# First values loaded from the ScalarE queue, the second batch's casts between the output weights, and the first output blocks three at a time

## The chip, the core and the metric

The kernel runs on one core of a Trainium2 chip. The metric is the device time of one execution in microseconds. Five engines run side by side, each through its own instructions in a fixed order: TensorE (PE in the rows; its weight loads are PEld), VectorE (DVE), ScalarE (ACT), GpSimd (POOL) and SyncE (SP). They wait for one another, and for DMA transfers, through semaphores. A transfer is issued by an instruction that stands in the order of the engine that issues it.

## The reference

Attention over 8 batches, 8 heads, 576 positions and 64 values per head: heads 0 to 3 see the last 32 positions, heads 4 to 7 every fourth of the last 128. Then a two-layer network on the 4608 rows of 512.

```python
scores = scale * np.matmul(q, k.transpose(0, 1, 3, 2))
mask_plain = (rel >= 0) & (rel < window)
mask_dil = (rel >= 0) & (rel < window * dilation) & (rel % dilation == 0)
scores = np.where(masks[None, :, :, :], scores, -1000000000.0)
attn = np.exp(scores); attn = attn / (np.sum(attn, axis=-1, keepdims=True) + 1e-09)
out = np.matmul(attn, v)
...
h = x @ w_in
g = h * (1.0 / (1.0 + np.exp(-beta * h)))
return (g @ w_out).astype(np.float32)
```

## The kernel before

The work is written in the order in which each engine gets it; nothing reorders it. A **batch** is brought in by steps that run on DMA. `cast_qk` (issued by GpSimd) reads q or k as float32 and writes a bfloat16 copy to a scratch in memory. `load_dil` and `load_plain` (issued by SyncE) read that copy transposed into `kdT`, `qdT` (heads 4 to 7), `kpT`, `qpT` and `opT` (heads 0 to 3). `load_vd` (2 transfers) and `load_vp` (8 to 10 transfers) bring the values as float32 into `vd_st` and `vp_st`, of which there is one each, and `cast_v` copies them into `vd` and `vp`. `spread_dil`, `spread_k` and `spread_q` copy the transposed q and k into the zero-padded tiles `qzd`, `kz` and `qq`.

The **attention** of a batch is a list of 33 steps, `STEPS`. `S` steps are scores and their exponential (`pt`, ScalarE, line 291), `V` steps are the product with the values and its division (PE line 307, VectorE lines 310 and 314), and `X` steps transpose the result into `xT` (PE line 323, ScalarE lines 329 and 333). The first figure behind the letter is the pair of heads: 2 and 3 are the dilated heads, whose steps come first; 0 and 1 are the plain ones. V00 is the first step that reads `vp`, V20 the first that reads `vd`. For batches 0 and 1 the mask is added on PE as a first matmul; from batch 2 on GpSimd multiplies it in after the exponential (line 293).

The **network** runs over 9 tiles of 512 rows, t = 0 to 8, in slots. `slot_h(t, fb)` is four 512-column matmuls, a tanh on ScalarE (line 351) and a product on VectorE (line 354) that gives `g`. `slot_o(t, tb, part)` is four of the sixteen 512-column matmuls of the output block `tb`; after part 3 ScalarE copies the block to `osb` (line 382) and SyncE stores it two slots later. Tile t = 0 uses batch 0 alone, and after its 16 h slots come its 16 o slots, block by block. The attention of batch t + 1 is laid between the slots of tile t: `FROM[t]` is the first slot behind which steps may stand, and slots weigh 1 (h) or 2 (o), except the last two, which weigh nothing. `extras(b)` hangs the loads and spreads of a batch on steps of the attention of batch b.

Hardware DMA transfers take eight semaphores in turn, and a ninth transfer waits until the first has landed; the transfers that GpSimd issues have eight of their own. Of PSUM's eight banks `psum_at` has five, `psum_h` two and `psum_o` one, and the `osb` pool has two buffers.

The start of the program before is written out by hand:

```python
    cast_v(0, 1, G)
    for n in range(2):
        spread_dil(0, n, nc.vector)
        spread_k(0, n, G)
    cast_v(0, 0, G)
    for g in range(4):
        load_w_in(g)
    for g in range(4):
        load_w_out(g)
```

After it come the steps of batch 0, then `build_beta`, then the casts and loads of batch 1.

## Time and profile before

| | us |
|---|---|
| median of 3 runs | 374.37 (373.09 to 481.56) |
| profiled execution, its own time | 375.59 |
| span of its trace | 373.9 |
| PE busy in the span | 315.0 (84%) |
| VectorE, ScalarE, GpSimd busy | 207.5, 189.7, 129.8 |

The trace is of one execution. Times in it are counted from the start of the span, and some 1.7 us of the execution lie outside the span. PEclk in a table by windows is the clock granted to TensorE as a share of 2.4 GHz: 1.00 is 2.4 GHz and 0.50 is 1.2 GHz. The share of busy time is an average over stages with different limits, so the stages are looked at one by one.

### The profile page before, as it was taken

What the parts mean: (1) busy time and instruction counts of PE and PEld (TensorE: products, weight loads), DVE (VectorE), ACT (ScalarE), POOL (GpSimd) and SP (SyncE); (2) the same over time, 40 slices, a digit from 0 to 9 for tenths busy, and PEclk for the clock granted to TensorE, in tenths of its full rate; (3) what the DMA queues carried; (4) which work ended last, traced back from release to release, by engine and by line L of the source; (5) the groups of instructions that cost most, each with busy time, mean ns of one, the idle gap of its engine ahead of it and who ended that gap; (6) DMA issues with size and microseconds to landing.
All of it is one profiled execution on the core that took longest, in us unless ns stands there. A gap on an engine that the chain in (4) does not pass through costs nothing.

```text
span 373.9 us, 5943 instructions
## 1 busy us (share of the span) xinstructions
PE 315.0 (84%) x2173; PEld 162.2 (43%) x2173; DVE 207.5 (55%) x421; ACT 189.7 (51%) x360; POOL 129.8 (35%) x162
## 2 busy tenths in 40 slices
PE   0267997487469499989999998999899999999995
PEld 0144443253235245545554554555455544444442
DVE  4353650644698827955894698479555634425400
ACT  1164652055446247656665675566566645535511
POOL 8837100210545634465355346424453300000000
PEclk9995899769989879999999999999999999999999
DMA  7948999899989779249927983996100110010022
GB/s 134 222 111 134 199 223 216 197 177 179 218 151 220 148 160 240 66 95 174 251 62 156 169 220 79 176 212 157 38 24 27 34 52 29 28 58 29 28 72 70
DMA packets 91262, 48.93 MB, mean 131 GB/s; under 512 B 74832, under 2 KB 86112, under 8 KB 90720
## 3 DMA queue, kind: packets, MB, share of 16 engines
q1 hardware_dynamic: 86176, 34.91, 41.6%
q0 software_dynamic: 5056, 13.63, 20.5%
q8 instruction: 17, 0.28, 0.3%
q14 instruction: 13, 0.11, 0.1%
HBM read 40.89 MB, written 18.87 MB: 160 GB/s over the span
## 4 chain that ended last, share of the span: by engine, by line
PE 55%; DVE 19%; DMA 11%; SPq 6%; ACT 3%; issue 2%; POOL 1%; DVEq 0%; ACTq 0%; POOLq 0%
PE h_ps L346 24%; PE o_ps L377 23%; DMA qk<-in_q_dram 7%; DVE qq L224 5%; DVE g L354 5%; DVE xs L314 4%; DVE kz L216 3%; SPq L237 2%; DMA w_in_bf<-in_moe_w_in_dram 2%; ACT tnh L351 2%; PE h_ps L377 2%; PE at L323 2%; SPq L203 2%; PE at L307 2%; SPq L192 1%
## 5 line engine op out<-in xcount | busy, mean ns | idle before, releaser
L354 DVE SCALAR_TENSOR_TENSOR g<-tnh,h_ps 128x512 bf16<-128x512 bf16 x134 | 91.3, 684 | 95.4 <-ACT tnh L351 95.3
L377 PE MATMUL o_ps<-w_out_bf,g 128*128 128x512 bf16 x544 | 139.0, 386 | 4.9 <-ACT osb L382 4.9
L346 PE MATMUL h_ps<-xT,w_in_bf 128*128 128x512 bf16 x536 | 137.3, 386 | 6.7 <-DVE g L354 5.7
L351 ACT ACTIVATE tnh<-h_ps,beta_half 128x512 bf16<-128x512 f32 x134 | 92.1, 687 | 64.8 <-PE h_ps L346 62.3
L346 PEld LDWEIGHTS <-w_in_bf 128*128 128x128 bf16 x576 | 54.0, 100 | 61.5 <-issue 12.7
L377 PEld LDWEIGHTS <-g 128*128 128x128 bf16 x576 | 53.5, 99 | 59.5 <-issue 9.4
L291 ACT ACTIVATE pt<-at 128x288 bf16<-128x288 f32 (+1 forms) x112 | 48.7, 443 | 42.6 <-PE at L285 30.1
L293 POOL TENSOR_TENSOR pt<-pt,mask_d 128x288 bf16<-128x288 bf16 x48 | 34.8, 733 | 55.3 <-ACT pt L291 55.3
L314 DVE TENSOR_TENSOR xs<-at,rcp 72x256 bf16<-72x256 f32 (+1 forms) x96 | 44.6, 465 | 13.2 <-PE at L323 8.9
L382 ACT ACTIVATE osb<-o_ps 128x512 f32<-128x512 f32 x34 | 20.3, 597 | 39.1 <-PE o_ps L377 32.5
L293 POOL TENSOR_TENSOR pt<-pt,mask_PP 128x384 bf16<-128x384 bf16 x24 | 24.2, 1008 | 34.1 <-ACT pt L291 34.0
L307 PEld LDWEIGHTS <-pt 128*128 128x128 bf16 x448 | 26.3, 103 | 22.0 <-issue 8.4
L253 POOL CAST vd<-vd_st 128x2048 bf16<-128x2048 f32 x8 | 16.1, 2013 | 44.2 <-DMA vd_st<-in_v_dram 44.2
L323 PE MATMUL at<-ident_b,xs 72*128 72x72 bf16 (+1 forms) x224 | 20.1, 210 | 13.0 <-DVE xs L314 5.5
L307 PE MATMUL at<-vd,pt 128*128 128x65 bf16 x256 | 19.8, 202 | 6.1 <-POOL vd L253 3.6
L285 PEld LDWEIGHTS <-kdT 128*128 128x128 bf16 x128 | 13.2, 106 | 27.1 <-issue 16.5
L323 PEld LDWEIGHTS <-xs 72*128 72x128 bf16 (+1 forms) x224 | 14.1, 103 | 22.5 <-DVE xs L314 12.6
L285 PE MATMUL at<-qzd,kdT 128*128 128x144 bf16 x128 | 19.9, 244 | 4.3 <-DVE qzd L212 4.3
L310 DVE RECIPROCAL rcp<-at 72x4 f32<-72x4 f32 (+1 forms) x96 | 17.0, 178 | 11.3 <-PE at L307 10.4
L329 ACT COPY xT<-at 128x288 bf16<-128x288 bf16 x32 | 12.6, 399 | 17.8 <-PE at L323 17.7
L271 PE MATMUL at<-neg_d,ident_b 128*128 128x288 bf16 x16 | 6.1, 385 | 14.7 <-DVE neg_d L154 14.7
L277 PE MATMUL at<-qq,kz 128*128 128x96 bf16 x192 | 16.7, 212 | 1.2 <-ACT qq L224 1.1
(63 smaller groups left out, 197.6 us busy)
## 6 DMA issues: line engine op xcount, KB each, us to landing
vp_st<-in_v_dram SPq DMA_DIRECT2D x62, 96.0 KB, 4.0
vd_st<-in_v_dram SPq DMA_DIRECT2D x8, 512.0 KB, 5.9
qk<-in_k_dram POOLq DMA_DIRECT2D x6, 576.0 KB, 5.9
qk<-in_q_dram POOLq DMA_DIRECT2D x6, 576.0 KB, 8.9
vd_st<-in_v_dram SPq DMA_DIRECT2D x8, 384.0 KB, 4.7
w_in_bf<-in_moe_w_in_dram POOLq DMA_DIRECT2D x4, 512.0 KB, 8.3
w_out_bf<-in_moe_w_out_dram POOLq DMA_DIRECT2D x4, 512.0 KB, 16.3
out_dram<-osb SPq DMA_DIRECT2D x8, 256.0 KB, 2.7
```

The costliest lines, as they stand in the source:

```text
L224: copy_on(eng)(out=qq[b % 2][rows, :, :, e], in_=raw[b, kind][rows, c0:c0 + 2 * S].rearrange("p (h i u) -> p h i u", h=4, i=NI))
L285: nc.tensor.matmul(sc[:, a, 0:2 * n], lhsT=kd[b][:, rp, h4, hf * (CT - P):hf * (CT - P) + P], rhs=qzd[b % 2][:, :, rp, h4, hf * HT:(hf + 1 ...
L291: nc.scalar.activation(out=w, in_=sc[:, :, 0:2 * n], func=ACT.Exp, scale=SCALE)
L293: nc.gpsimd.tensor_tensor(out=w, in0=w, in1=mask, op=ALU.mult)
L307: nc.tensor.matmul(pv[:, a, h2, :], lhsT=pt[x][:, c:c + P], rhs=rhs, start=True, stop=True)
L314: nc.vector.tensor_tensor(out=xs_t[b, x, jx][:, a0:a0 + m], in0=pv[0:n, :, :, 0:D], in1=rcp[0:n, 0:m].unsqueeze(3).to_broadcast([n, m, 2, ...
L323: nc.tensor.transpose(xp[:, a * n:(a + 1) * n], xs[:, a].rearrange("p h d -> p (h d)"), ident_b[0:n, 0:n])
L346: nc.tensor.matmul(hps, lhsT=w_in_bf[:, kt, fb * P:(fb + 1) * P], rhs=xT[:, kt, t * NTOK:(t + 1) * NTOK], start=(kt == 0), stop=(kt == NKT ...
L351: nc.scalar.activation(out=tnh[:], in_=hps, func=ACT.Tanh, scale=beta_half[:, fb:fb + 1])
L354: nc.vector.scalar_tensor_tensor(out=g[:], in0=tnh[:], scalar=1.0, in1=hps, op0=ALU.add, op1=ALU.mult)
L377: nc.tensor.matmul(ops[:], lhsT=g_t[t, fb][:, tb * P:(tb + 1) * P], rhs=w_out_bf[:, fb, :], start=(fb == 0), stop=(fb == NFB - 1))
L382: nc.scalar.mul(out=osb[:], in_=ops[:], mul=0.5)
```

## The change

The loads of batch 0's values and of `beta` are issued by ScalarE ahead of its first activation. The dilated half of batch 0's values is cast by VectorE. The dilated masks are built before the plain ones, and four memsets of `kz` go from GpSimd to VectorE. Two of the four groups of `w_in` are issued before the cast of `vp`. The values of batch 1 are loaded ahead of its transposes, and its q and k are cast between the second and third group of `w_out`. The first three output blocks of t = 0 run part by part, in the two banks of `psum_h` and the one of `psum_o`. `FROM` goes from 26 to 27 and from 5 to 8, `osb` from two buffers to four, and the rows of `vp` and `vd` from 96 to 66 elements. Batch 2's casts stand behind a one-element GpSimd copy that reads batch 1's `opT`, at V22 instead of V31, and its loads at V23 instead of X31.

```diff
-    FROM = {0: 26, 1: 5}
-    DV = 96
+    FROM = {0: 27, 1: 8}
+    DV = D + 2
...
-    osb_pool = pool("osb", 2)
+    osb_pool = pool("osb", 4)
...
-            nc.gpsimd.memset(kz[i][64:128, :, :, 0], 0.0)
-            nc.gpsimd.memset(kz[i][0:64, :, :, 1], 0.0)
+            nc.vector.memset(kz[i][64:128, :, :, 0], 0.0)
+            nc.vector.memset(kz[i][0:64, :, :, 1], 0.0)
...
-            if t == NTT - 1 and tb % 2:
+            if t == NTT - 1 and tb % 2 or t == 0 and tb < 2:
                 o_t[t, tb] = psum_h.tile([P, HD], FP32, name="h_ps")
...
+            if b == 1:
+                at("V22", wait_raw, 1)
             for kind in "kq":
-                at("S20" if b > 1 else "V31", cast_qk, b + 1, kind)
+                at("S20" if b > 1 else "V22", cast_qk, b + 1, kind)
             for kind in "kq":
-                at("V21" if b > 1 else "X31", load_dil, b + 1, kind)
+                at("V21" if b > 1 else "V23", load_dil, b + 1, kind)
...
+    def wait_raw(b):
+        G.tensor_copy(out=gate_t[0:1, 0:1], in_=raw[b, "o"][0:1, 0:1])
...
+    load_vd(0, A)
+    load_vp(0, A)
+    A.dma_start(out=beta_row[:], in_=moe_beta.rearrange("(f p) -> f p", p=P))
     make_identity(nc, ident_b[:])
+    build_masks_d()
+    build_masks_p()
     zeros()
...
+    cast_v(0, 1, V)
+    for n in range(2):
+        spread_dil(0, n, V)
+        spread_k(0, n, G)
+    finish_masks_p()
     make_identity(nc, ident_f[:])
...
+    for g in range(2):
+        load_w_in(g)
     cast_v(0, 0, G)
-    for g in range(4):
+    for g in range(2, 4):
         load_w_in(g)
...
+    load_vd(1, SQ)
+    load_vp(1, SQ)
+    for g in range(2):
+        load_w_out(g)
+    for h in (4, 0):
+        for kind in "kq":
+            cast_qk(1, kind, h, 4)
+    for g in range(2, 4):
+        load_w_out(g)
...
+        if t == 0:
...
+            left = [(slot_o, 0, tb, part) for part in range(4) for tb in range(3)] + left[12:]
```

The order of ScalarE's instructions at the start of the program shows the first two parts of this. Names in brackets are semaphores that an instruction waits for: DMAHW0 to DMAHW7 are the eight of the hardware queues, DMASW0 to DMASW7 those of GpSimd's transfers. Before:

```order
L109 ACT_TABLE_LOAD
L109 ACTIVATE warm<-warm 128x1 [waits DVE_49]
L291 ACTIVATE pt_115<-at 128x288 [waits PE_49] x4
L291 ACTIVATE pt_116<-at 128x288 [waits PE_49] x3
L224 COPY qq_109<-qpT 64x24x48 [waits DMAHW5_49]
```

ScalarE loaded its table at once and had nothing else ahead of the first exponential. The same engine in the changed program, from the seventh of its thirteen transfers on:

```order
L245 DMA vp_st<-in_v_dram 64x6x64 [waits DMAHW2_49]
L245 DMA vp_st<-in_v_dram 64x6x64 [waits DMAHW4_49]
L245 DMA vp_st<-in_v_dram 64x6x64 [waits DMAHW5_49]
L245 DMA vp_st<-in_v_dram 64x6x64 [waits DMAHW6_49]
L245 DMA vp_st<-in_v_dram 64x6x64 [waits DMAHW7_49]
L245 DMA vp_st<-in_v_dram 64x6x64 [waits DMAHW0_49]
L442 DMA beta_row<-in_moe_beta_dram 16x128 [waits DMAHW1_49]
L112 ACT_TABLE_LOAD
L112 ACTIVATE warm<-warm 128x1 [waits DVE_49]
L295 ACTIVATE pt_115<-at 128x288 [waits PE_49] x4
```

Thirteen transfers, the table load and the warm-up now stand ahead of the first exponential. The semaphores are shared with SyncE's transposes: DMAHW4 was last taken by `qdT`, DMAHW7 by `kpT` and DMAHW1 by `qpT`, so the transfer of `beta` waits until `qpT` has landed.

GpSimd's order, from the cast of `vp` on, before:

```order
L164 DMA w_in_bf<-in_moe_w_in_dram 128x4x512 x4
L169 DMA w_out_bf<-in_moe_w_out_dram 128x4x512 [waits DMASW0_49]
L169 DMA w_out_bf<-in_moe_w_out_dram 128x4x512 [waits DMASW1_49]
L169 DMA w_out_bf<-in_moe_w_out_dram 128x4x512 [waits DMASW2_49]
L169 DMA w_out_bf<-in_moe_w_out_dram 128x4x512 [waits DMASW3_49]
L180 DMA qk_463<-in_k_dram 16x9216 [waits DMASW4_49]
L180 DMA qk_463<-in_q_dram 16x9216 [waits DMASW5_49]
L180 DMA qk_463<-in_k_dram 16x9216 [waits DMASW6_49]
L180 DMA qk_463<-in_q_dram 16x9216 [waits DMASW7_49]
```

And in the changed program, from the third and fourth group of `w_in` on:

```order
L172 DMA w_in_bf<-in_moe_w_in_dram 128x4x512 x2
L177 DMA w_out_bf<-in_moe_w_out_dram 128x4x512 [waits DMASW0_49]
L177 DMA w_out_bf<-in_moe_w_out_dram 128x4x512 [waits DMASW1_49]
L188 DMA qk_226<-in_k_dram 16x9216 [waits DMASW2_49]
L188 DMA qk_226<-in_q_dram 16x9216 [waits DMASW3_49]
L188 DMA qk_226<-in_k_dram 16x9216 [waits DMASW4_49]
L188 DMA qk_226<-in_q_dram 16x9216 [waits DMASW5_49]
L177 DMA w_out_bf<-in_moe_w_out_dram 128x4x512 [waits DMASW6_49]
L177 DMA w_out_bf<-in_moe_w_out_dram 128x4x512 [waits DMASW7_49]
```

The four casts of batch 1 moved ahead of the last two groups of `w_out`, so these two land after them.

## Rows read from the trace of the kernel before

**Rows 1.** Busy time by stage (window, length, then each engine's busy us and instructions).

```profile
core 0: us, PE busy (x) PEld busy (x) DVE busy (x) ACT busy (x) POOL busy (x), PEclk, DMA share, GB/s
0.00:17.08 17.08, 0.40 (x2) 0.21 (x2) 6.70 (x26) 1.49 (x2) 13.99 (x30) 1.00 0.91 173
...
29.05:34.57 5.52, 4.22 (x55) 3.31 (x54) 3.06 (x9) 3.20 (x8) 5.52 (x8) 0.56 0.83 122
34.57:50.84 16.27, 16.26 (x64) 6.80 (x65) 9.54 (x14) 10.07 (x15) 2.50 (x6) 0.83 1.23 201
50.84:62.24 11.40, 10.03 (x47) 4.39 (x45) 2.19 (x5) 2.12 (x4) 0.00 (x0) 1.00 1.10 203
62.24:87.30 25.06, 16.02 (x160) 10.51 (x158) 10.95 (x31) 8.93 (x23) 4.41 (x5) 0.80 0.94 196
...
96.56:133.67 37.11, 25.94 (x197) 13.38 (x197) 28.57 (x48) 15.58 (x33) 21.06 (x23) 0.89 0.87 177
```

**Rows 2.** Waits of PE, 0 to 134 us: us in total, times, longest us.

```profile
PE at L285 <- DVE qzd L212: 4.3, 2, 2.3
...
PE at L307 <- POOL pt L293: 2.5, 2, 2.1
```

**Rows 3.** Timeline of the opening (start, length, engine, line; in brackets the idle time before).

```profile
0.80 1.28 ACT L109 ACT_TABLE_LOAD   x1 [0.80 <-PEq L512]
...
4.73 0.91 DVE L119 MEMSET vd_st<- 32x1024 f32 x1 [0.25 <-issue]
...
14.35 2.46 SPq L203 DMA_TRANSPOSE qpT<-qk  x1
...
17.52 1.85 ACT L291 ACTIVATE pt<-at 128x288 bf16<-128x288 f32 x4 [15.21 <-PE at L285]
...
25.02 0.61 SPq L438 DMA_DIRECT2D beta_row<-in_moe_beta_dram  x1
...
28.95 3.03 POOL L164 DMA_DIRECT2D w_in_bf<-in_moe_w_in_dram  x4
29.05 0.34 PE L307 MATMUL at<-vp,pt 128*128 128x65 bf16 x6 [3.34 <-POOL vp L251]
```

**Rows 4.** DMA issues: the q transpose issued at 14.35 us, the last weight issued by 34.2 us.

```profile
qpT<-qk SPq DMA_TRANSPOSE x1, 4.8
...
w_in_bf<-in_moe_w_in_dram POOLq DMA_DIRECT2D x1, 512.0 KB, 5.6
...
w_out_bf<-in_moe_w_out_dram POOLq DMA_DIRECT2D x1, 512.0 KB, 19.0
```

**Rows 5.** Chain that ended last, in order of time: sixteen 512-column matmuls back to back.

```profile
359.06 3.45 PE h_ps L377 x16
```

**Rows 6.** Timeline of the second batch's attention: the waits and what ends them.

```profile
67.15 0.30 PE L307 MATMUL at<-vd,pt 128*128 128x65 bf16 x4 [3.65 <-POOL vd L253]
...
68.43 1.91 PE L377 MATMUL o_ps<-w_out_bf,g 128*128 128x512 bf16 x4
...
72.07 4.36 SPq L366 DMA_DIRECT2D out_dram<-osb  x5
...
75.03 0.60 ACT L382 ACTIVATE osb<-o_ps 128x512 f32<-128x512 f32 x1 [5.94 <-DMA out_dram<-osb]
...
75.97 0.40 PE L323 MATMUL at<-ident_b,xs 72*128 72x72 bf16 x4 [4.55 <-ACT pt L291]
```

**Rows 7.** Timeline of the third batch's start: slots of t = 1, VectorE copy and GpSimd queue.

```profile
66.29 1.79 DVE L216 COPY kz<-kpT 64x1536 bf16<-64x1536 bf16 x2 [3.86 <-DMA kpT<-qk]
...
89.83 1.89 PE L346 MATMUL h_ps<-xT,w_in_bf 128*128 128x512 bf16 x8 [0.64 <-DVE g L354]
...
92.34 1.89 PE L346 MATMUL h_ps<-xT,w_in_bf 128*128 128x512 bf16 x8 [0.63 <-DVE g L354]
...
97.38 1.89 POOL L253 CAST vd<-vd_st 128x2048 bf16<-128x2048 f32 x1 [20.96 <-DMA vd_st<-in_v_dram]
...
100.19 5.68 DVE L216 COPY kz<-kpT 64x1536 bf16<-64x1536 bf16 x2
```

More of the change, by code (lines that the diff above doesn't have):

```diff
@@ L108, in zeros @@
         nc.vector.memset(warm[:], 0.0)
+        nc.vector.memset(vd_st[96:128, 0], 0.0)
+        for e in range(2):
+            nc.vector.memset(vp_st[64 * e:64 * e + WIN // 2, 0, 0], 0.0)
         nc.scalar.activation(out=warm[:], in_=warm[:], func=ACT.Exp)
@@ L114, in zeros, with negate, build_masks_d, build_masks_p @@
             nc.vector.memset(qzd[i][0:64, 1], 0.0)
-            nc.gpsimd.memset(kz[i][64:128, :, :, 0], 0.0)
-            nc.gpsimd.memset(kz[i][0:64, :, :, 1], 0.0)
+            nc.vector.memset(kz[i][64:128, :, :, 0], 0.0)
+            nc.vector.memset(kz[i][0:64, :, :, 1], 0.0)
             nc.vector.memset(vp[i][:, :, :, D:D + 1], 1.0)
             nc.vector.memset(vd[i][:, :, :, :, D:D + 1], 1.0)
-        nc.vector.memset(vd_st[96:128, 0], 0.0)
-        for e in range(2):
-            nc.vector.memset(vp_st[64 * e:64 * e + WIN // 2, 0, 0], 0.0)
-    def build_masks():
-        pp = mask_p["PP"]
+    def negate(n, m):
+        nc.vector.tensor_scalar(
+            out=neg[n][:], in0=m, scalar1=-1.0, scalar2=NEG, op0=ALU.add, op1=ALU.mult)
+    def build_masks_d():
+        for hf, lo in ((0, 0), (1, HT - 16)):
+            flat = mask_d[hf][:].rearrange("p a b n -> p (a b) n")
+            nc.gpsimd.memset(flat, 1.0)
+            nc.gpsimd.affine_select(
+                out=flat, in_=flat, pattern=[[0, 4], [1, HT]], base=lo,
+                channel_multiplier=-1, compare_op=ALU.is_ge, fill=0.0)
+            nc.gpsimd.affine_select(
+                out=flat, in_=flat, pattern=[[0, 4], [-1, HT]], base=WIN - 1 - lo,
+                channel_multiplier=1, compare_op=ALU.is_ge, fill=0.0)
+            negate(f"d{hf}", mask_d[hf][:].rearrange("p a b n -> p a (b n)"))
+    def build_masks_p():
+        pp, fp = mask_p["PP"], mask_p["FP"]
         for e in range(2):
@@ L236, in load_vp, with load_vd @@
                 if b or h4:
[L237 removed]
+                    eng.dma_start(out=dst, in_=src(0, 0))
                 else:
[L239 to L242 removed]
+                    eng.dma_start(out=dst[:, 1:NI], in_=src(1, 0))
+                    eng.dma_start(out=dst[WIN // 2:64, 0:1], in_=src(0, WIN // 2))
+    def load_vd(b, eng):
         rows = v[b, 4:8].rearrange("h (t T) d -> t h (T d)", T=C)
         st = vd_st[:].rearrange("p f h T d -> p f h (T d)")
[L245 to L246 removed]
+        eng.dma_start(out=st[0:96, 0], in_=rows[0:96])
+        eng.dma_start(out=st[:, 1], in_=rows[16:CT])
     def cast_v(b, h, eng):
@@ L452 @@
             for n in range(4):
-                spread_q(0, n, nc.vector if n % 2 else nc.scalar)
+                spread_q(0, n, V if n % 2 else A)
         attention_step(0, name)
     build_beta()
-    for h in (4, 0):
-        for kind in "kq":
-            cast_qk(1, kind, h, 4)
     for kind in "kq":
         load_dil(1, kind)
-    load_vd(1)
     for kind in "kqo":
         load_plain(1, kind)
-    load_vp(1)
     at_once = [4, 2] + [1] * (NTT - 3) + [4]
```

63 lines of the change are left out of this document (18 added, 45 removed).

## The prediction, made before the changed kernel ran

> **What bounds the kernel now.** I read the table by stages first, since 84% busy on PE hides where it is idle. From 134 us on PE is near its bound and the change touches little there; what can be won lies before. The table [rows 1] shows four places. Batch 0's attention ends with 5.52 us at a PEclk of 0.56. The h slots of t = 0 take 16.27 us at 0.83, so part of them runs at 1.2 GHz. The stretch from 62.24 to 87.30, batch 1's attention, holds only 16.02 us of PE work in 25.06. The attention of batch 2 takes 37.11 us with PE at 25.94 and VectorE at 28.57.
>
> The timelines then say what ends each wait. In batch 0, V00 starts 3.34 us late because `vp` is cast late [rows 3]; its loads stand last on SyncE's queue, and `beta`, behind them, is issued at 25.02. In batch 1 PE waits 3.65 us for the cast of `vd`, and then 4.55 us in a longer chain [rows 6]: PE waits for an exponential, which stands on ScalarE behind an `osb` copy, which waits 5.94 us for a store of an earlier block, and that store, at 72.07, was queued on SyncE behind the loads of `vp`. In batch 2 PE waits for `qzd` (4.3 us in two waits over this whole stretch, the longest 2.3) and 2.1 us for GpSimd's masking [rows 2], because GpSimd's queue stood still for 20.96 us until `vd_st` had landed at 97.38 [rows 7].
>
> **The change part by part.** I write A to E for five stages in order of time, a minus for time won.
>
> *A, to the first h slot (34.57 before).* Moving the values to ScalarE's queue takes V00's wait away but puts a new one in. ScalarE is an in-order engine: its first exponential now stands behind thirteen transfers, and the last of them, `beta`, waits until `qpT` has landed; then come the table load of 1.28 us and the warm-up. Before, the table was loaded at 0.80 and the first exponential ran at 17.52 [rows 3]. `qpT` was issued at 14.35 and landed 4.8 us later, at 19.15 [rows 3, 4]. Two `vd` issues leave SyncE's queue ahead of it; at the 0.61 us of a like issue [rows 3] that is 1.2 us, so 17.9. Against that the values now share the DMA engines with the casts from the start. At most all 0.77 MB of `vp` get ahead of `qpT`, at the opening's 173 GB/s [rows 1] 4.4 us, so 22.3. I take 18.5, near the lower end, since `vd` had stood ahead of `qpT` before too. With the issue of `beta` (0.61) and the table load (1.28) ScalarE is free at 20.4, 2.9 us later than the old first exponential (2.3 to 6.7). VectorE is not later: its memsets grow by four at 0.9 us each (the nearest row is the 0.91 of `vd_st`, rows 3) and by a cast that takes GpSimd 1.89 [rows 7]; from the masks at an estimated 7 us through 5.1 us of old memsets this ends near 18.5 with the spreads.
>
> V00 could have run at 29.05 less 3.34, at 25.7; 2.9 later is 28.6, 0.4 earlier than now. So of the 3.3 us almost all is given back. The tail from 29.05 to 34.57 is 5.52 us of which PE worked 4.22 at 0.56; GpSimd now issues `w_in` before the cast of `vp`, some 8 us earlier, so nothing waits for weights, and I take 0.9 off. A is -1.3, between -2.3 and +4.
>
> *B, the sixteen h slots.* PE's low clock followed the idle 3.3 us. Without that I expect 2.4 GHz: sixteen matmuls take 3.45 us [rows 5], a slot of four 0.863, sixteen slots 13.8 against 16.27. B is -2.5, between -2.5 and 0.
>
> *C, the output blocks up to the attention of batch 1.* Three blocks in three banks need no wait for an `osb` copy between them. Twelve parts are 12 x 0.863 = 10.4 us, against 11.40 for eleven parts with their gaps. C is -1.0. Its risk is the weights, since the last two groups of `w_out` come after the four casts. Before, the first group landed 5.6 us after its issue at 28.95, and the eighth 19.0 after its issue at 34.2 [rows 3, 4], so seven groups took 18.6 us, 2.66 each. A cast of half the heads is 288 KB beside the 512 of a group, 1.5 us. `w_in` is now issued when GpSimd has copied `kz`, near 20.4 (`kpT` at 17 and about 3 us), so the first group lands at 26.0 and the last at 26.0 + 18.6 + 4 x 1.5 = 50.6. Batch 1's values, 1.66 MB at the weights' rate (1.05 MB of float32 in 2.66 us), add up to 4.2: 54.8. The last round needs it at 33.3 + 13.8 + 9 x 0.863 = 54.9. So it is just in time; each us that the weights are later costs one. C is between -1.0 and +4. The transposes of batch 1 start when its first cast lands (44 with all delays); the first two are in by 44 + 2 x 2.46 + 4.8 = 53.7, before 57.5, where S20 now stands.
>
> *D, the attention of batch 1 with the last o slots (25.06).* Its values are loaded some 25 us ahead, so the 3.65 go. With four `osb` buffers no copy of t = 0 waits for a store, so the 4.55 go. One o slot that cost 1.91 at the low clock [rows 6] is counted in C now. 25.06 less 10.1 leaves 15.0. What comes late next is the chain of the steps itself. Three `osb` copies ahead of the exponentials may cost 0.6 each, and the slots at full clock may win 1 us each: D is -10.1, between -8.3 and -12.
>
> *E, tile t = 1 (87.30 to 133.67, 46.4 us).* `FROM` at 8 puts three more h slots ahead of the attention. Alone, two slots take 2.51 us (89.83 to 92.34, rows 7), so three cost 3.8, less 3 x 0.69 of VectorE time that leaves the crowded part: +1.7. Batch 2's casts wait only for `opT` of batch 1, near 57 to 61, not for the late cast of `vp`, so the 2.3 us for `qzd` go; and with `vd_st` early GpSimd's queue is empty when masking starts, so the 2.1 go. E is -2.7, between +2 and -7. The rest, t from 2 on, stays as it is; narrower `vp` rows are read by the same matmuls, and I put them at nothing.
>
> The sum is -1.3 - 2.5 - 1.0 - 10.1 - 2.7 = -17.6. From the profiled execution's own 375.6 us that gives 358. That execution is 1.2 us above the median of 374.4, a spread I leave in the range.
>
> **Where the skill and the rows meet.** The table copies of `kz` on VectorE took 5.68 us for batch 2 and 1.79 for batch 1 [rows 7], the slow ones while GpSimd masked its backlog. The Trainium skill, page "SBUF — State Buffer", section "Who interferes with whom", says that a VectorE copy in a two-port mode and a GpSimd instruction exclude each other for whole instructions; the trace agrees as far as it goes. By that rule an empty GpSimd queue would also give back the 3.9 us between the two rows, and the sum would be 354.
>
> The first values now come over another engine's queue, and the opening's DMA share is already 0.91 [rows 1]. The Trainium skill, page "DMA: Bandwidth & Descriptors", section "Issuing engines are not separate DMA queues", says that issuing from several engines saves only sequencer time, since all share the same 16 engines. By that rule the move alone gains no bandwidth and could only shift what waits; my A, where 0.4 of 3.3 us is left, is of that kind.
>
> **The rivals.** *Weights late.* If GpSimd's `w_in` issue slips by 3 us or the casts and transposes share worse, PE waits in the third and fourth round of C, 4 us, and after such a wait the clock may fall as it did after 3.34 us: 1.9 instead of 0.86 for some slots. That costs C 5 and D 1 or so: 364. For it speaks that the margin is 0.1 us; against it that the first round of blocks needs only the first group.
>
> *ScalarE held longer.* If `qpT` lands at 22.3, the first exponential runs at 24.2, A is +2.5 and the weights, issued after `kz`, move with it: 362 to 365. For it speaks the shared DMA in the opening; against it that SyncE's own queue got shorter.
>
> *VectorE's copies run free.* `kz` and `qq` of batch 2 at their short times, as the 1.79 of batch 1: E is -6.6, 354. Against it: GpSimd still masks each exponential there.
>
> *Slower.* One mechanism could turn the sign: ScalarE's hold with no bound. Each us that `qpT` lands later delays the first exponential, and with it everything, by one. The gain is used up when `qpT` lands 17.6 us later than I take, at 36; with all 2.6 MB of both batches' values ahead of it at 173 GB/s (15 us) and SyncE's issues stretched with them it would land at 38 to 42, and the time is 378 to 382. Against it: batch 1's values stand behind `opT` on SyncE.
>
> *It doesn't do what it says.* V00's wait may only move from `vp` to ScalarE; I hold this for most of A already. If PE then idles long enough at the start of the attention to lose the clock again, B is 0 as well: 361.
>
> **How the numbers follow.** I give my sum 0.55, weights late 0.14, ScalarE held longer 0.12, copies running free 0.10, the clock lost again 0.05, slower 0.04. The range goes from 351 (free copies and D at its end) to 367 (weights late and ScalarE held together). A measurement of this kernel tells about 2% from no change, 7.5 us: below 366.9 is faster. Only the two middle rivals together, and the slower one, come above: faster 0.87, same 0.09, slower 0.04. I predict 358.
>
> **What would show it.** In the changed profile: the first exponential near 20.4, ending a wait of ScalarE that goes back to `beta` and `qpT`; no wait for `vp` at V00; h slots of t = 0 at 0.863; `o_ps` and `h_ps` blocks without gaps, S20 of batch 1 near 58; no wait for `vd` or a store behind it, t = 1 beginning near 72.5; t = 1 in 44 us. If the first exponential is past 24, or PE waits for `w_out_bf`, or t = 1 takes over 48, the step named there is wrong.

## The result, and the profile after

The changed kernel takes 360.36 us (median of 4 runs, 359.55 to 360.58) against 374.44 us before: a ratio of 0.963 (95% interval 0.960 to 0.966), 14.1 us less. The prediction was 358, in a range of 351 to 367. The profiled run took 360.58 us with a span of 358.9; before it was 375.6 and 373.9.

The table of stages of the changed kernel, cut at the marks that [rows 1] has for the kernel before:

```profile
core 0: us, PE busy (x) PEld busy (x) DVE busy (x) ACT busy (x) POOL busy (x), PEclk, DMA share, GB/s
...
34.61:48.60 13.99, 13.99 (x65) 6.24 (x65) 9.80 (x15) 10.63 (x16) 3.50 (x4) 1.00 1.22 216
48.60:60.47 11.87, 10.68 (x49) 4.68 (x48) 1.55 (x3) 1.91 (x4) 1.47 (x1) 1.00 1.14 187
60.47:74.61 14.14, 12.16 (x155) 8.26 (x154) 10.56 (x32) 9.15 (x23) 1.42 (x4) 1.00 0.94 164
...
88.06:118.37 30.31, 21.59 (x185) 11.63 (x185) 24.55 (x45) 13.37 (x30) 17.64 (x20) 0.92 0.97 190
```

Against [rows 1], stage by stage (before, after, difference, my term):

| stage | before | after | difference | predicted |
|---|---|---|---|---|
| A, to the first h slot | 34.57 | 34.61 | 0.0 | -1.3 |
| B, sixteen h slots of t = 0 | 16.27 | 13.99 | -2.3 | -2.5 |
| C, output blocks to S20 of batch 1 | 11.40 | 11.87 | +0.5 | -1.0 |
| D, attention of batch 1 | 25.06 | 14.14 | -10.9 | -10.1 |
| E, tile t = 1 | 46.37 | 43.76 | -2.6 | -2.7 |
| sum | | | -15.3 | -17.6 |

What follows t = 1 takes 240.5 us against 240.2. So the gain lies where I put it, mostly in D. The stages miss the forecast sum by 2.3 us: A and C fall short by 2.8 together, since the opening won nothing and the output blocks became longer, B and E by 0.3, and D gives 0.8 more than I forecast. In this table C ends, as in [rows 1], with the mask matmul that opens S20 (60.47); the table of all runs below takes the matmul behind it (61.26).

The timeline of the opening after the change, ScalarE's queue, GpSimd, VectorE and PE (start, length, engine, line; the idle time before and what ended it in brackets):

```profile
4.68 0.33 ACTq L248 DMA_DIRECT2D vp_st<-in_v_dram  x1
...
14.03 5.02 ACTq L245 DMA_DIRECT2D vp_st<-in_v_dram  x6
...
19.74 1.28 ACT L112 ACT_TABLE_LOAD   x1 [19.74 <-DMA vp_st<-in_v_dram]
21.14 1.29 ACT L295 ACTIVATE pt<-at 128x288 bf16<-128x288 f32 x4
...
25.21 1.50 POOL L259 CAST vp<-vp_st 128x1536 bf16<-128x1536 f32 x1 [3.11 <-DMA vp_st<-in_v_dram]
25.30 1.72 DVE L232 COPY qq<-opT 64x1152 bf16<-64x1152 bf16 x1
27.17 0.33 PE L281 MATMUL at<-qq,kz 128*128 128x96 bf16 x4 [2.04 <-ACT xT L337]
...
30.22 0.53 PE L311 MATMUL at<-vp,pt 128*128 128x65 bf16 x6
```

The reader is to see three things. ScalarE's queue stands between 5.01 and 14.03, and its first exponential comes at 21.14 (17.52 before, [rows 3]), as forecast behind the transfers and the table load. V00 no longer waits for `vp`, but starts at 30.22, later than the 29.05 before. And between the two, VectorE's copy of `opT` takes 1.72 us while GpSimd casts `vp` beside it, PE stands 2.04 us (its row names ScalarE's `xT`, but the matmul reads `qq`, whose last copy ends at 27.02), and the granted clock from 26 to 34 us is 0.79, a mean between the two levels.

Batch 1, from the transposes to the start of its scores, answers to [rows 6]:

```profile
46.80 7.41 SPq L200 DMA_TRANSPOSE kdT<-qk  x1
...
50.26 1.02 PE L381 MATMUL h_ps<-w_out_bf,g 128*128 128x512 bf16 x4 [0.63 <-DVE g L358]
...
54.32 3.51 SPq L200 DMA_TRANSPOSE qdT<-qk  x1
...
57.88 1.89 PE L381 MATMUL h_ps<-w_out_bf,g 128*128 128x512 bf16 x8 [0.55 <-DMA w_out_bf<-in_moe_w_out_dram]
...
60.29 0.92 DVE L220 COPY qzd<-qdT 64x1152 bf16<-64x1152 bf16 x2 [10.08 <-DMA qdT<-qk]
...
61.26 0.28 PE L289 MATMUL at<-qzd,kdT 128*128 128x144 bf16 x2 [0.51 <-DVE qzd L220]
```

The waits of 3.65 for `vd` and of 4.55 behind the store are gone; no wait of PE between 62 and 74.61 is longer than 0.46. In their place stand two short waits that both end with a transfer: 0.55 us for the last output weights and 0.51 for `qzd`, whose source `qdT` landed just before. The chain that ended last goes through the same transposes, here with its lengths in time order:

```profile
29.59 17.19 DMA qk<-in_k_dram
...
57.92 3.73 DMA kpT<-qk
```

Between the two lines stand the issues of `kdT` and `qdT`, and behind `kpT` its copies to `kz`. From 29.59 to 61.65 the chain runs through transfers and their issues alone: the casts take 17 us beside the weights, and the issue of one transpose 7.41 us. PE's sixteen slots and twelve parts lie beside it and end only 0.5 us before `qzd` is there.

Batch 2, which answers to [rows 2, 7]:

```profile
87.09 0.91 DVE L220 COPY qzd<-qdT 64x1152 bf16<-64x1152 bf16 x2
87.74 2.01 POOL L261 CAST vd<-vd_st 128x2048 bf16<-128x2048 f32 x1 [21.61 <-DMA vd_st<-in_v_dram]
88.06 0.41 PE L289 MATMUL at<-qzd,kdT 128*128 128x144 bf16 x4 [2.33 <-DMA vp_st<-in_v_dram]
90.69 5.29 DVE L224 COPY kz<-kpT 64x1536 bf16<-64x1536 bf16 x1
90.69 2.78 POOL L297 TENSOR_TENSOR pt<-pt,mask_d 128x288 bf16<-128x288 bf16 x4
91.49 0.27 PE L311 MATMUL at<-vd,pt 128*128 128x65 bf16 x3 [1.04 <-POOL pt L297]
```

PE still waits 2.33 us at S20 (the row puts it down to a load of values; the run with `qzd` early below shows that it is `qzd`, and the repeated kernel's row names it), GpSimd's queue still stands 21.61 us for `vd_st`, and one `kz` copy still takes 5.29 us. Only the wait for the masking fell, from 2.1 to 1.04. E came out at its size here with other pieces than mine.

### The profile page after: what moved, and what is told of

Its sections match the earlier page's. It is cut to its first block, busy times and chain, and to the rows that moved or that the text cites. A ratio compares the mean times of both kernels' runs of the same rounds, so it can differ in the third digit from the quotient of the medians.

```text
span 358.9 us, 5941 instructions
## 1 busy us (share of the span) xinstructions
PE 308.4 (86%) x2173; PEld 159.2 (44%) x2173; DVE 212.6 (59%) x426; ACT 189.6 (53%) x360; POOL 122.3 (34%) x158
## 4 chain that ended last, share of the span: by engine, by line
PE 53%; DVE 20%; DMA 14%; SPq 5%; ACT 3%; issue 2%; POOL 1%; ACTq 1%; DVEq 0%; POOLq 0%
PE o_ps L381 23%; PE h_ps L350 23%; DMA qk<-in_k_dram 7%; DVE qq L232 5%; DVE g L358 5%; DVE xs L318 5%; DVE kz L224 4%; SPq L200 3%; DMA vp_st<-in_v_dram 3%; DMA qdT<-qk 3%; PE h_ps L381 2%; DVE rcp L314 2%; PE at L327 2%; PE at L311 1%; PE at L289 1%
## 5 line engine op out<-in xcount | busy, mean ns | idle before, releaser
L381 PE MATMUL o_ps<-w_out_bf,g 128*128 128x512 bf16 x512 | 129.5, 381 | 3.2 <-ACT osb L386 3.2
L381 PEld LDWEIGHTS <-g 128*128 128x128 bf16 x576 | 52.7, 98 | 57.9 <-issue 6.6
L297 POOL TENSOR_TENSOR pt<-pt,mask_PP 128x384 bf16<-128x384 bf16 x24 | 23.3, 972 | 35.9 <-ACT pt L295 35.8
L386 ACT ACTIVATE osb<-o_ps 128x512 f32<-128x512 f32 x32 | 19.1, 597 | 26.3 <-PE o_ps L381 26.2
L289 PE MATMUL at<-qzd,kdT 128*128 128x144 bf16 x128 | 19.2, 240 | 15.6 <-DVE qzd L220 13.2
L327 PE MATMUL at<-ident_b,xs 72*128 72x72 bf16 (+1 forms) x224 | 19.2, 202 | 6.3 <-ACT xT L333 3.2
L261 POOL CAST vd<-vd_st 128x2048 bf16<-128x2048 f32 x7 | 14.4, 2050 | 24.3 <-DMA vd_st<-in_v_dram 24.3
L259 POOL CAST vp<-vp_st 128x1536 bf16<-128x1536 f32 x8 | 12.7, 1585 | 22.2 <-issue 16.5
L220 DVE COPY qzd<-qdT 64x1152 bf16<-64x1152 bf16 x16 | 13.7, 858 | 10.9 <-DMA qdT<-qk 10.7
```

Source lines behind the costliest of these rows:

```text
L289: nc.tensor.matmul(sc[:, a, 0:2 * n], lhsT=kd[b][:, rp, h4, hf * (CT - P):hf * (CT - P) + P], rhs=qzd[b % 2][:, :, rp, h4, hf * HT:(hf + 1 ...
L297: nc.gpsimd.tensor_tensor(out=w, in0=w, in1=mask, op=ALU.mult)
L327: nc.tensor.transpose(xp[:, a * n:(a + 1) * n], xs[:, a].rearrange("p h d -> p (h d)"), ident_b[0:n, 0:n])
L381: nc.tensor.matmul(ops[:], lhsT=g_t[t, fb][:, tb * P:(tb + 1) * P], rhs=w_out_bf[:, fb, :], start=(fb == 0), stop=(fb == NFB - 1))
L386: nc.scalar.mul(out=osb[:], in_=ops[:], mul=0.5)
```

## The experiments

Marks of all runs, in us from the start of the span (first h slot; first q times k matmul of batch 1, called S20 here; begin of t = 1; the same matmul of batch 2; begin of t = 2), with median and ratio to the kernel before on the same chip. The marks are of one profiled execution each; with the values on SyncE it took 369.48 us and with the three edits together 366.16, 2.9 and 3.8 us above the median. The kernel before has medians of 373.2 to 374.4 in the four sets of runs, so medians of different rows compare to about 1 us:

| run | h slots | S20, batch 1 | t = 1 | S20, batch 2 | t = 2 | median | ratio (95%) |
|---|---|---|---|---|---|---|---|
| before | 34.58 | 62.48 | 87.30 | 96.56 | 133.46 | 374.44 | 1 |
| changed | 34.61 | 61.26 | 74.61 | 88.06 | 118.37 | 360.36 | 0.963 (0.960-0.966) |
| changed, again | 34.49 | 60.73 | 74.01 | 88.94 | 119.50 | 360.33 | 0.966 (0.962-0.970) |
| values on SyncE | 39.13 | 66.38 | 79.56 | 93.00 | 123.68 | 366.57 | 0.982 (0.976-0.988) |
| table load first | 32.66 | 61.32 | 74.72 | 89.76 | 117.66 | 360.65 | 0.968 (0.962-0.973) |
| casts last | 32.69 | 61.71 | 75.64 | 90.51 | 121.85 | 362.52 | 0.972 (0.967-0.977) |
| casts first | 33.38 | 60.67 | 74.03 | 87.48 | 120.16 | 360.82 | 0.965 (0.961-0.969) |
| vp late | 34.29 | 59.56 | 72.92 | 86.37 | 119.49 | 362.57 | 0.971 (0.968-0.973) |
| block by block | 32.29 | 66.76 | 80.05 | 93.49 | 123.84 | 366.13 | 0.981 (0.975-0.987) |
| two osb buffers | 34.65 | 60.45 | 78.50 | 104.17 | 134.85 | 377.96 | 1.012 (1.008-1.016) |
| from slot 5 | 34.70 | 60.84 | 74.14 | 83.40 | 118.24 | 361.41 | 0.967 (0.964-0.970) |
| qzd early | 34.63 | 60.69 | 74.13 | 85.08 | 116.32 | 358.87 | 0.960 (0.957-0.963) |
| qzd and kz early | 32.68 | 60.84 | 74.08 | 85.03 | 117.39 | 359.65 | 0.962 (0.957-0.966) |
| together | 32.48 | 59.43 | 74.15 | 85.10 | 122.11 | 362.34 | 0.973 (0.968-0.977) |

**The queue of the first values.** The values and `beta` go back to SyncE's queue, at their old places; all else stays as changed.

```diff
-    load_vd(0, A)
-    load_vp(0, A)
-    A.dma_start(out=beta_row[:], ...)
...
+    load_vd(0, SQ)
     for kind in "kqo":
         load_plain(0, kind)
+    load_vp(0, SQ)
+    SQ.dma_start(out=beta_row[:], ...)
```

> The changed kernel with batch 0's values and beta issued by SyncE again, at their old places between and behind the transposes. Theory of the hold (the ScalarE queue trades one wait for another): the first exponential comes back from 21.1 to about 19, V00 waits about 3 us for vp again, and the first h slot stays within 0.5 us of 34.6; since PE idles there, its clock falls and the h slots of t = 0 take about 16 instead of 14.0 us, so some 362.5 us. Rival (the queue itself brings bandwidth): the first h slot comes 3 us later and the time is about 365. If neither the start of the h slots nor the clock moves: 360.

All marks from the first h slot on come 4.5 to 5.3 us later, and the median is 6.2 us above the changed kernel's. GpSimd's queue and PE's V00 show why:

```profile
32.03 1.46 POOL L259 CAST vp<-vp_st 128x1536 bf16<-128x1536 f32 x1 [9.24 <-DMA beta_row<-in_moe_beta_dram]
...
33.55 0.49 PE L311 MATMUL at<-vp,pt 128*128 128x65 bf16 x6 [4.06 <-POOL vp L259]
...
36.37 0.55 POOL L188 DMA_DIRECT2D qk<-in_k_dram  x1
```

The cast of `vp` stands between two pairs of `w_in` groups, and GpSimd waits 9.24 us before it. Behind it on the same queue are half of `w_in`, all of `w_out` and the casts of batch 1, which begin at 36.37 instead of 29.59. The DMA share from 20 to 40 us is 0.98 instead of 1.22 (175 GB/s instead of 211): the engines had less to do. PE waits 4.06 us for `vp` at V00, where I had about 3, and starts it at 33.55 instead of 30.22; the h slots take 15.6 us (39.13 to 54.69), where I had 16. What I had wrong is the other side: the first exponential comes at 21.48, no earlier than behind the hold (21.14), so nothing makes up for the late values. So ScalarE's queue is worth some 5 us, on two paths that both start with the late `vp`: V00's wait, and GpSimd's queue, which releases weights and casts later. At S20 they end within 0.3 us of each other (PE waits 0.25 us there), and this run doesn't tell them apart. The Trainium skill, page "DMA: Bandwidth & Descriptors", section "Issuing engines are not separate DMA queues", says that another issuing engine saves only sequencer time; the rows don't speak against that for the bandwidth, but the moment at which `vp` is issued, and what GpSimd's queue holds back until it lands, are what the 5 us come from.

**The table load first.** The warm-up stands at the head of ScalarE's queue, only `vd` and the first quarter of `vp` are loaded from it, the rest and `beta` from SyncE behind the transposes.

```diff
+    nc.vector.memset(warm[:], 0.0)
+    nc.scalar.activation(out=warm[:], in_=warm[:], func=ACT.Exp)
     load_vd(0, A)
-    load_vp(0, A)
-    A.dma_start(out=beta_row[:], ...)
+    load_vp(0, A, range(1))
...
+    load_vp(0, SQ, range(1, 4))
+    SQ.dma_start(out=beta_row[:], ...)
```

> The changed kernel with ScalarE freed: table load and warm-up ahead of its transfers, only six transfers left on it, and the rest of vp and beta on SyncE behind the transposes. Theory of the sum (stages add up): the first exponential moves from 21.1 to about 19.4, the h slots begin 1.5 to 1.8 us earlier and the time is about 358.6. Rival (the DMA chain of casts and transposes sets batch 1's S20): the h slots begin earlier, but S20 of batch 1 stays at 60.4 behind qdT and the time stays at 360.0 to 360.5.

ScalarE is free from 2.3 us on here, and still the first exponential comes at 20.55, where I had 19.4:

```profile
16.71 3.35 DVE L218 COPY qzd<-qdT 64x1152 bf16<-64x1152 bf16 x2
...
20.55 1.85 ACT L293 ACTIVATE pt<-at 128x288 bf16<-128x288 f32 x4 [18.25 <-PE at L287]
```

It waits for PE's scores, and these wait for VectorE's two `qzd` copies, which take 3.35 us beside GpSimd's `kz` copies (0.91 before the change, where those came later). In nine of the ten runs whose opening is that of the changed kernel these copies end at the same time, and the first exponential comes at 20.57 to 20.97; only in the first profile of the changed kernel (copies 2.08 us, exponential at 21.14) was ScalarE clearly the last. So the hold on ScalarE cost 0.4 us at most in those nine.

The h slots begin at 32.66, 2 us earlier than in that profile, but this isn't shown to be the edit's work: three runs with the unaltered opening begin between 32.29 and 32.69 too. At S20 of batch 1 nothing is left of it (61.32 against 61.26). PE waits in the rounds of blocks instead, 1.96 and 0.72 us for `w_out_bf`, and 0.62 for `qzd`. The transfers bind this stretch, and my step that adds the opening's saving to the sum falls.

**The casts behind all weights, and ahead of all.** The four casts of batch 1 stand behind the last two groups of `w_out`, or ahead of the first two.

```diff
     for g in range(2):
         load_w_out(g)
-    for h in (4, 0):
-        for kind in "kq":
-            cast_qk(1, kind, h, 4)
     for g in range(2, 4):
         load_w_out(g)
+    for h in (4, 0):
+        for kind in "kq":
+            cast_qk(1, kind, h, 4)
```

> The changed kernel with the four casts of batch 1 behind all four groups of w_out again. Theory that the place of the casts is what wins: they land about 5 us later (kdT issued near 52 instead of 46.8), qdT lands about 5 us later and so does S20 of batch 1, about 365 us. Rival (transposes beside weights are slow, 7.4 and 3.5 us of issue, and would be fast behind them): kdT and qdT take about 2 us each, qdT lands near 60 as before, and the time stays at 360.

> The four casts of batch 1 are issued ahead of all output weights instead of between them, the rest as changed. Theory that the chain of transfers sets S20 of batch 1: kdT starts near 39 instead of 46.8, stays slow beside the weights (some 7 us for each of the first two), qdT is in by 54, and S20 comes when the three blocks are done, at 59 to 59.5: 1 to 2 us won. Rival: the output weights, now behind the casts as a whole, end later and the rounds of blocks wait for them: 0 to 3 us lost.

SyncE's transposes and VectorE's first copy with the casts last:

```profile
54.04 2.38 SPq L200 DMA_TRANSPOSE kdT<-qk  x1
...
60.73 0.92 DVE L220 COPY qzd<-qdT 64x1152 bf16<-64x1152 bf16 x2 [12.84 <-DMA qdT<-qk]
```

and the same with the casts first:

```profile
44.04 9.63 SPq L200 DMA_TRANSPOSE kdT<-qk  x1
...
59.70 0.92 DVE L220 COPY qzd<-qdT 64x1152 bf16<-64x1152 bf16 x2 [11.12 <-DMA qdT<-qk]
```

The transpose of `kdT` is issued 10 us apart and takes 2.38 us behind the weights, 7.41 among them and 9.63 ahead of more of them; the copy that needs `qdT` comes at 60.73, 60.29 and 59.70. With the casts last PE is through with its blocks at 57.44, since the weights are early, and then waits 3.98 us for `qzd`; with the casts first it waits for weights (0.56 and 0.84). The order moves the wait from one consumer to the other and shifts S20 by about 1 us. In the median the casts last are 2.2 us above the changed kernel and the casts first the same.

**Fewer bytes ahead.** If the order is worth so little, the bytes that have to be through before `qdT` should decide. The plain values of batch 1, 0.79 MB, go behind its transposes.

```diff
     load_vd(1, SQ)
-    load_vp(1, SQ)
...
     for kind in "kqo":
         load_plain(1, kind)
+    load_vp(1, SQ)
```

> The load of the plain values of batch 1 (0.79 MB) stands behind the five transposes of batch 1 on SyncE's queue instead of ahead of the output weights, the rest as changed. Theory: what sets S20 of batch 1 is how many bytes the DMA engines move before qdT, casts, weights, values and transposes in whatever order; 0.79 MB less is 2.0 us at the weights' rate, so qdT is in 1.5 to 2.5 us earlier and S20 comes at 58.5 to 59.5, or at the end of the blocks of outputs if that is later; 1 to 2 us won, vp still in time. Rival 1: the transposes are slow by their own form and follow the casts, not the bytes: 0. Rival 2: vp now comes late at V00 of batch 1 and gives it back with the stores behind it: 0 to +3.

The first copy and S20 do what the theory said, from SyncE's and VectorE's rows of this run:

```profile
43.28 1.75 SPq L200 DMA_TRANSPOSE kdT<-qk  x1
45.15 5.56 SPq L200 DMA_TRANSPOSE qdT<-qk  x1
...
56.92 0.92 DVE L220 COPY qzd<-qdT 64x1152 bf16<-64x1152 bf16 x2 [7.03 <-DMA qdT<-qk]
```

The copy comes 3.4 us earlier than in the changed kernel, more than the 2.0 us that the bytes cost at the weights' rate. PE waits for neither weights nor `qzd`; S20 is at 59.56, directly behind the blocks, and t = 1 begins 1.1 to 1.7 us earlier than in the two runs of the changed kernel. But the time is not better: 362.57 (362.30 to 362.73) against 360.33 (359.10 to 363.70) for the changed kernel on the same chip. The rows of batch 2 tell where it went:

```profile
66.11 1.47 POOL L259 CAST vp<-vp_st 128x1536 bf16<-128x1536 f32 x1 [26.36 <-DMA vp_st<-in_v_dram]
67.64 0.53 POOL L188 DMA_DIRECT2D qk<-in_k_dram  x1
...
90.19 2.18 POOL L261 CAST vd<-vd_st 128x2048 bf16<-128x2048 f32 x1 [21.39 <-DMA vd_st<-in_v_dram]
93.54 2.78 POOL L297 TENSOR_TENSOR pt<-pt,mask_d 128x288 bf16<-128x288 bf16 x4
94.34 0.35 PE L311 MATMUL at<-vd,pt 128*128 128x65 bf16 x3 [3.44 <-POOL pt L297]
```

`vp` is not late for V00 of batch 1, but its cast, at 66.11 instead of 58.22, stands ahead of batch 2's casts on GpSimd. These start at 67.64 instead of 64.89, `vd` of batch 2 is cast 2.5 us later, the masking starts 2.9 us later, and PE waits 3.44 us for it instead of 1.04. So the lead is gone by t = 2 (119.49, against 118.37 and 119.50 in the two runs of the changed kernel); the span is 2 us longer (361.0 against 358.9 and 359.1), and that difference arises at and behind t = 2, where its cause is open. My rival had the right kind of loss and the wrong place.

**Block by block.** The slots of the first three blocks of t = 0 stand in the old order, one block after the other, in the same three banks.

```diff
-            left = [(slot_o, 0, tb, part) for part in range(4) for tb in range(3)] + left[12:]
```

> The changed kernel with the output blocks of t = 0 in the old order, block by block, in the same banks. Theory that the rounds hide the late weights: the first block needs the last group of w_out at about 51, but it lands near 57.5; PE waits about 6 us, S20 of batch 1 comes at about 66 instead of 60.5, and the clock falls after the wait: 365 to 368. Rival (the banks alone do it, the order is free because qdT holds S20 at 60.4 anyway): within 1 us of 360.4.

PE's rows, where the blocks meet the weights:

```profile
53.80 1.86 PE L381 MATMUL h_ps<-w_out_bf,g 128*128 128x512 bf16 x4 [6.03 <-DMA w_out_bf<-in_moe_w_out_dram]
...
57.20 6.15 PE L381 MATMUL h_ps<-w_out_bf,g 128*128 128x512 bf16 x20 [1.53 <-DMA w_out_bf<-in_moe_w_out_dram]
```

The first block needs all four groups of `w_out` within 3.5 us, so PE waits 7.6 us in two pieces and S20 comes at 66.76, 5.5 us late. The rounds need one group each 2.6 us and hide 5 to 6 us of the weights' arrival. Without them the time is 5.8 us above the changed kernel's.

**Two buffers for the copied blocks.**

```diff
-    osb_pool = pool("osb", 4)
+    osb_pool = pool("osb", 2)
```

> Two buffers for the copied output blocks instead of four, the rest as changed. My theory of D: the copy of the third block of t = 0 (60.67 in the changed kernel) must now wait until the store of the first has landed; that store is issued at 62.38, behind five transposes on SyncE's queue, so ScalarE stands until about 65 and the exponentials of batch 1 with it: h slots of t = 1 begin 3 to 4.5 us later than 74.61, the time is 3 to 4.5 us longer. Rival: the stretch is bound by the transposes and by the steps' own chain, and a late copy is hidden: 0 to +1.

The time is 377.96 us, slower than the kernel before: 17.6 us more than the changed kernel, where I had 3 to 4.5. ScalarE, SyncE and PE in this run:

```profile
64.70 0.60 ACT L386 ACTIVATE osb<-o_ps 128x512 f32<-128x512 f32 x1 [5.04 <-DMA out_dram<-osb]
...
86.11 5.79 SPq L370 DMA_DIRECT2D out_dram<-osb  x6
90.46 0.60 ACT L386 ACTIVATE osb<-o_ps 128x512 f32<-128x512 f32 x1 [13.09 <-DMA out_dram<-osb]
92.41 3.96 PE L350 MATMUL h_ps<-xT,w_in_bf 128*128 128x512 bf16 x10 [12.02 <-DVE g L358]
```

The first wait is the one that I expected: t = 1 begins 3.9 us later. The second I had not seen: the copy of the last block of t = 0 waits 13.09 us for a store that stands on SyncE's queue behind batch 2's transposes and values and is issued from 86.11 on; the Tanh of the lone h slots stands behind that copy, and PE behind the Tanh. The new order of loads without the buffers is a loss.

**The lone slots of t = 1.** Batch 2's attention is spread from slot 5 on, as before the change, instead of from slot 8.

```diff
-    FROM = {0: 27, 1: 8}
+    FROM = {0: 27, 1: 5}
```

> The attention of batch 2 is spread from slot 5 of t = 1 on, as before the change, instead of from slot 8; the rest as changed. My sum gave the three further lone slots +1.7, so by it this kernel is 1.7 us faster than the changed one. Rival: the lone slots buy time for the transposes and values of batch 2 to land, and S20 at 82 to 83 meets late data (qdT is issued at 74.68, vd at 80.70 to 81.3 in the changed kernel): 1 to 4 us slower, with waits for vd or POOL's masking in place of the lone slots.

S20 of batch 2 comes 4.7 us earlier and t = 2 at the same time (118.24 against 118.37). PE waits 3.53 us for GpSimd's masking, which cannot start before the cast of `vd`. The time is that of the changed kernel within the intervals. Neither my +1.7 nor a loss of the rival's size is shown: the slots only fill a time in which batch 2's data are on the way.

**The copies of batch 2 ahead of the crowd.** The two `qzd` copies are issued after the seventh lone slot; in a second kernel they are issued after the fifth, and the two `kz` copies after the seventh.

```diff
             fn(*args)
+            if t == 1 and n == 6:
+                for i in range(2):
+                    spread_dil(2, i, V)
```

> The two copies of qzd for batch 2 are issued after the seventh lone h slot of t = 1 instead of at S20, the rest as changed. Theory: the 2.33 us that PE waits at S20 of batch 2 are VectorE's order (qdT had landed some 7 us earlier, the copies stand behind the g of the last lone slot), so the wait goes and 1 to 2.3 us with it. Rival: the stretch up to t = 2 is bound by VectorE's or ScalarE's whole work, and the wait only moves: 0, between -0.5 and +0.5.

> Both the copies of qzd and of kz for batch 2 are issued among the lone h slots of t = 1 (after the fifth and the seventh), where GpSimd is idle, the rest as changed. Theory of the shared access: without GpSimd's masking beside it the first kz copy takes some 0.6 to 1.1 us instead of 5.29; the qzd wait (2.33) and the wait of an h slot for g (3.15) go, 4 to 6 us in all, and t = 2 begins at 112 to 114 instead of 118.4. Rival: kz is slow for its own reason (a 64-partition copy with strides beside transposes in flight), or its 5 us were hidden by other waits: 1 to 2 us, as for the qzd copies alone.

With `qzd` early S20 of batch 2 waits for nothing:

```profile
84.08 0.92 DVE L220 COPY qzd<-qdT 64x1152 bf16<-64x1152 bf16 x2
85.08 0.41 PE L289 MATMUL at<-qzd,kdT 128*128 128x144 bf16 x4
...
90.71 0.27 PE L311 MATMUL at<-vd,pt 128*128 128x65 bf16 x3 [2.80 <-POOL pt L297]
```

So the 2.33 us were VectorE's order, as the theory had it, and not a late transfer. S20 is 3.0 us earlier, t = 2 begins 2.1 us earlier, and the span is 1.7 us shorter; the wait for the masking grows from 1.04 to 2.80. The ratio, 0.960, lies below the two of the changed kernel (0.963 and 0.966), but the intervals overlap: 1 to 2 us, not settled.

With `kz` early too, the copies run while GpSimd is idle:

```profile
84.04 1.12 DVE L224 COPY kz<-kpT 64x1536 bf16<-64x1536 bf16 x2
```

Each takes 0.56 us, where one took 5.29 beside GpSimd's masking. The theory of the shared access is borne out for the length of the copy. It fails for the time: S20 to t = 2 takes 32.36 us, against 31.24 in the kernel that moves `qzd` alone (whose `kz` copies took 2.30 together), PE waits 2.38 us for the masking, and nothing is gained over that kernel. The run from slot 5 says the same, with 1.66 us for both copies and t = 2 where it was. In the first profile PE waits 3.15 us for a `g` that stands behind the slow copy, but with the copy short the masking, which waits for the cast of `vd`, takes its place.

**The changed kernel again, and three edits together.** The table load first, `vp` of batch 1 late and `qzd` of batch 2 early in one kernel, with the unaltered changed kernel beside it.

> The changed kernel once more, unaltered, as the anchor for the three others on this chip: a ratio between 0.960 and 0.967 to the kernel before, S20 of batch 1 within 0.7 us of 60.5 wherever the first h slot starts (32.5 to 34.6).

> Three edits on the changed kernel: the table load and warm-up at the head of ScalarE's queue with only vd and the first quarter of vp on it, the plain values of batch 1 behind its transposes, and the qzd copies of batch 2 among the lone h slots. If the opening (2 us) and the bytes ahead of qdT (2 us) have to be eased together, S20 of batch 1 comes at 57 to 58.5, and with the qzd wait gone t = 2 begins 4 to 5 us earlier: 355 to 357. Rival: each pulls only on a link that another one holds: 358 to 360.

The repeated kernel is where it was (360.33), with S20 of batch 1 at 60.73 as expected. It also bears on the slow copy, by VectorE's rows of batch 2:

```profile
92.31 0.88 DVE L224 COPY kz<-kpT 64x1536 bf16<-64x1536 bf16 x1
...
94.48 1.12 DVE L224 COPY kz<-kpT 64x1536 bf16<-64x1536 bf16 x1
```

The same program took 5.29 and 0.56 us for these two copies in its first profile, 3.9 us more, and S20 to t = 2 is 30.3 us there and 30.6 here. The granted clock of that stretch is 0.92 there and 0.84 here, so the two are not a clean pair.

The three together take 362.34: the h slots begin at 32.48, S20 of batch 1 comes at 59.43, and PE still waits 1.52 us for `w_out_bf` in the third round and 1.27 for `vp` at V00, so t = 1 begins no earlier than in the changed kernel (74.15). In batch 2 the cast of `vd` comes at 91.17, 3.4 us later than in the changed kernel, and PE waits 6.86 us for the masking (this profile is the slowest of the kernel's six executions). The rival holds: each edit eases a link that another one holds. No version here is shown to beat the changed kernel; the one with `qzd` early comes nearest.

## Why the prediction was right, and which terms were off

**A, mis-sized: -1.3 forecast, 0.0 measured.** V00's wait for `vp` went. The step that failed is "2.9 later is 28.6": V00 starts at 30.22. The tail behind it, from which I took 0.9 off, takes 4.4 us and not more than I had (4.6). What the sum lacks is the `qq` copies ahead of the plain scores. In the first profile GpSimd's cast of `vp` (25.21) meets them, one takes 1.72 us, PE stands 2.04 us, and the clock is 0.79 from 26 to 34 us. In the run with `kz` early, whose opening is the same code, the cast was at 22.88:

```profile
22.88 1.46 POOL L259 CAST vp<-vp_st 128x1536 bf16<-128x1536 f32 x1 [0.98 <-DVE xs L318]
25.37 0.68 DVE L232 COPY qq<-opT 64x1152 bf16<-64x1152 bf16 x1
26.66 0.33 PE L281 MATMUL at<-qq,kz 128*128 128x96 bf16 x4 [1.26 <-ACT qq L232]
```

There the copy took 0.68, the clock stayed at 1.00 (2.4 GHz), V00 started at 28.42, and the h slots began at 32.68, 1.9 us earlier. The ten runs with this opening fall into two kinds. In three the cast is all but over when the copies run; they take 0.71 us at most, and the first h slot is at 32.29 to 32.69. In seven the cast begins at 24.27 to 25.21, one copy takes 1.09 to 1.72, and the first h slot is at 33.38 to 34.70. In six of these seven the clock is 0.79. In the seventh (casts first) it stays at 1.00, though from 23 to 27 us the copies and casts agree with the repeated kernel's to 0.02 us; its first h slot is at 33.38, the repeated kernel's at 34.49, so the clock costs 1.1 us and the copies the rest. The opening thus won between 0 and 2.3 us, and my 33.3 lies in between. I had the rival that the clock is lost again at the start of the attention, but tied it to B, and it hit A.

The first exponential at 21.14, forecast 20.4, looks like a hit of the hold on ScalarE, but it is luck: with the table first ScalarE is free and the exponential comes at 20.55 all the same. "VectorE is not later" was the wrong step there: its `qzd` copies, which I had near 18.5, end at 18.8 in the first profile and at 20.1 in all others with this opening. The rival "slower" also counted too few bytes: by the sizes of their transfers the values of both batches are 3.3 MB, not 2.6.

**B, right:** 13.99 us at a clock of 1.00, forecast 13.8.

**C, mis-sized: -1.0 forecast, +0.5 measured.** The step "the last group at 26.0 + 18.6 + 4 x 1.5 = 50.6", with the values 54.8, was too early: PE met the last weights at 57.88. And "the first two are in by 53.7" was wrong by 6.5 us: `qdT` landed at 60.2. The transposes started at 46.80 and not at 44, and I priced two issues at 2.46 us each, from transposes in the opening, where beside the weights they took 7.41 and 3.51. In C itself the late weights cost 0.55 us, and another 0.63, at 50.26, is a wait that I had not counted: the second block takes the bank of the last h slot, which is free only when VectorE has made its `g`. The rival "weights late" was half true, at a tenth of its price, because the rounds of blocks absorb it. What the sum did not contain is that the stretch up to S20 has one bound, the transfers: with the first h slot 2 us earlier (table load first, `kz` early) S20 stays, with the casts elsewhere it shifts by 1 us, with 0.79 MB less it comes 1.2 to 1.7 us earlier and PE's blocks end last. My sum of A, B and C was thus a sum over a chain that is not the longest. Its sign survived because D, the largest term, lies behind it.

**D, right:** 14.14 us, forecast 15.0. That more than two buffers are needed is shown by the kernel with two (+17.6 us); of that 3.9 us fall into this stage. That the early load takes away the 3.65 us for `vd` is read from the rows; no run put that load back.

**E, right in size once, wrong in its pieces.** In the repeated kernel t = 1 takes 45.5 us (74.01 to 119.50), 0.7 less than before, while what follows is 0.9 us shorter than in the first profile; so the match of -2.6 with -2.7 is in part luck. The three lone slots cost nothing (from slot 5: same t = 2). The 2.33 us for `qzd` did not go, since not the late casts but VectorE's queue made them (`qzd` early). The masking wait gave 1.0 instead of 2.1. What did bring the 2.4 to 2.6 us of the first profile is open. One reading is: with the lone slots as before the change, the stretch from S20 of batch 2 to t = 2 takes 34.8 us instead of 36.9 to 37.1, and in it the last `qq` copies of batch 3 no longer meet GpSimd's casts. Before, two rows of VectorE, at 123.36 and 126.28, took 2.20 (one copy) and 1.85 us (two), beside GpSimd's casts at 123.35 and 125.89. After the change the same three copies take 1.02 and 0.91, and the cast comes behind them, at 114.75: 2.1 us less of VectorE's time. The repeated kernel speaks against it: there the cast, at 112.01, meets the last two copies again, they take 2.51, and S20 to t = 2 is 30.6 us all the same, even at the lower clock. No run moved that cast alone.

**The rival of free copies** (354 us) and the rule behind it: the Trainium skill, page "SBUF — State Buffer", section "Who interferes with whom", says that a VectorE copy in a two-port mode and a GpSimd instruction exclude each other, and the trace agrees, 0.56 us with GpSimd idle against 5.29 beside its masking. The price that I gave it, 3.9 us, was wrong: taken away, by an edit or in the repeated kernel, it gave nothing.

**Untried:** the early load of batch 1's `vd` by itself, three `osb` buffers, the gate that holds batch 2's casts until `opT` of batch 1 has landed, the narrower rows of `vp` and `vd`, and an order of GpSimd's queue in which batch 2's casts stand ahead of batch 1's cast of `vp`; the run with `vp` late suggests that the last is where E might still give something.

## What to carry to other kernels

Before adding up what stages save, ask for each stage end which chain it closes: where two or three chains (PE's slots, the transfers, another engine's queue) end within a us of each other, shortening one is worth only the gap to the next, as the opening's 2 us, the casts' place and the late `vp` show. An in-order queue that issues transfers is a chain of its own: look for the instruction on it that waits for data, and count what stands behind, transfers of the next stage and stores included (5 us here for late values and a cast that waits for them ahead of the weights, 17 us for a store behind the next batch's loads). When a transfer landed was told better here by the bytes ahead of it than by the order of the issues. And one profile is one draw: the same opening ended at 32.3 to 34.7 us, and the same t = 1 took 43.8 and 45.5, so look at a second one before a term is credited.
